# Three edits in a grouped-query attention and ResMLP kernel: twelve products moved from GpSimd to VectorE, two weight blocks sent through DRAM, one transpose placed a step later

## The chip, the cores and the metric

The kernel runs on one core of one Trainium2 chip. The metric is the device time of one execution in microseconds (us); the median of several executions is compared. The core's engines are TensorE (PE in the profile, with its weight loads as PEld), VectorE (DVE), ScalarE (ACT), GpSimd (POOL) and SyncE (SP). SP and POOL issue nearly all DMAs, each in its own order.

## The reference

Eight batches of 384 tokens. Attention has 16 query heads on 4 key and value heads of 64 elements; its output, 1024 wide, goes through a ResMLP block whose hidden layer is 4096 wide. The types in and out are float32.

```python
scores = scale * q @ k.T              # each query head on its group's key head
x = softmax(scores) @ v               # heads side by side: (8, 384, 1024)
a1 = alpha1 * x + beta1
tok = einsum('ts,bsd->btd', w_tok, a1)
u = x + lam * tok
a2 = alpha2 * u + beta2
ch = maximum(a2 @ w_ch1, 0) @ w_ch2   # (1024 x 4096), then (4096 x 1024)
out = u + lam * ch
```

## The kernel before, in words

**Pairs and products.** The batches are taken two at a time, in four pairs (`pair(i)`, L772). The two batches of a pair are the two block rows of a 2x2 block product, and each channel product is made of seven half-size products `o` = 1 to 7 instead of eight. The operands are sums and differences of blocks. `opb(k)` (L91) holds the left operands (turned activations and their sums, made by `sums_a`, L446, and at L850). `sum_w1(g, o)` (L506) makes the W1 operands on VectorE out of a left block `g` and a right block `g + 16`. The sums of W2 blocks are made once, in pair 0 (`sum_w2`, L496), written to DRAM as `w2s` (`keep_w2`, L493) and fetched by the later pairs (`fetch`, L525).

**Streams of weights.** A W1 block is 256 columns of W1, 512 KB as bf16. `load_w1` (L181) takes a free slot of the ring `w1` (six slots) and issues a DMA on POOL that casts float32 to bf16 on its way. `order1` (L439) is 0, 16, 1, 17, 2, 18 and so on: left and right blocks in turn. `queue` (L572 to L581) lists every load in order; `pump` (L534) issues the head of it each time `free` (L530) returns a slot. So a load is issued when the reader of an older block is through, in the queue's order alone.

**What runs in pair 0.** The attention of batches 0 and 1 comes first, then pair 0's first product (`first_product`, L641; matmuls at L681), then its second product (`second_product`, L728; matmuls at L752). The second product has 21 turns `(o, ms)`, a turn being 16 matmuls of 512 columns that end in one 128 x 512 accumulator, given out in four steps of four: 84 steps. While it runs, the attention of batches 2 and 3 is placed between its steps by hand: `plan` (L1069) says which calls follow which step of which product, `side(b)` (L214) gives the tables of one batch (L410 to L416), and batch 3's table is moved by 38 steps (L1122). Per pair of heads `p` these calls are `scores3` (scores at L260, exponentials on ACT at L269), `av` (matmuls at L295; on VectorE the reciprocal at L300, the division at L303 and the product with alpha1 and lam at L309), `tok_flip` (token mixing at L324 and L328; u at L331, a2 at L334; a store of u at L227) and, for batch 3, `turn` (L394: three transposes on TensorE at L398, copied by ACT at L400). Scores, `av`, `tok` and `turn` share three PSUM banks in rotation (`three`, L192), so each call waits until the reader of the bank three calls earlier is through.

**The order on the engines** is the program's order on each engine; nothing is reordered. A waiting instruction holds all behind it on its engine or queue.

**The lam products.** When a turn of the second product gives a finished 128 x 512 float32 block, `later` gets an entry; `flush` (L793) takes entries at later steps (L760 in the second product of pair 0, L845 in the next first product). An entry is `scaled` (L788): a `tensor_tensor` that multiplies the block in place with `lam_t` (L790) and a `store` (L441) that adds it to `out` by a DMA on POOL (L442). The multiply is on GpSimd in pair 0 (`lead`), twelve times, and on VectorE in the other pairs.

**After pair 0's second product** come pair 1's first product (matmuls at L831) and the rest in the same way. Group `g` of a first product needs W1 blocks `g` and `g + 16`. `home(c)` (L468) is a part of `arena` that holds block `c` of one quarter of W2 ("11") in pair 0's second product; its last readers are the turns of `o` = 7, which end with step 71, and the stretch is written again by pair 1's hidden units of group 6.

Of the kernel before, what the change touches and what calls it, by code (L numbers as in the profile page):

```python
# [13 lines left out]
def kernel(  # L14
# [21 lines left out]
    nc = tc.nc  # L36
# [82 lines left out]
    w2s = [tc.dram_tile([P, NDT * CW * P], bf, name=f"w2s{i}") for i in range(SLOTS)]  # L119
    PLACE2 = {o: i for i, o in enumerate((1, 2, 6, 5, 3, 7, 4))}  # L120
# [58 lines left out]
    w1_slots, w1_free = {}, list(range(RING))  # L179

    def load_w1(c):  # L181
        w1_slots[c] = w1_free.pop(0)
        nc.gpsimd.dma_start(out=w1[:, w1_slots[c]], in_=w1src[:, :, c * CW * P:(c + 1) * CW * P])  # L183
# [30 lines left out]
    def side(b):  # L214
# [197 lines left out]
        for p in range(NP):  # L412
            put((4, 10, 14, 18, 24, 29, 33, 35)[p], av, p)
            put((8, 15, 17, 22, 27, 32, 36, 38 if b % 2 else 39)[p], tok_flip, p)
            if by_pe(p):
                put(((13, 20, 22, 28, 34, 37, 40, 42) if b == 3 else (0, 0, 0, 0, 0, 36, 39, 41))[p], turn, p)  # L416
# [89 lines left out]
    def sum_w1(g, o):  # L506
        a, c = w1[:, w1_slots[g]], w1[:, w1_slots[g + NCH // 2]]
        H1, H2 = slice(0, NDT // 2), slice(NDT // 2, NDT)
        if o == 7:
            tt(out=c[:, H1], in0=c[:, H2], in1=c[:, H1], op=SUB)  # L510
            tb[g, 7], tb[g, 1], tb[g, 2], tb[g, 3] = c[:, H1], a[:, H1], a[:, H2], c[:, H2]
            return
        tb[g, o] = t = piece().rearrange("p (a c) -> p a c", a=NDT // 2)
        x, y = {5: (c[:, H1], a[:, H1]), 6: (c[:, H2], tb.get((g, 5))), 4: (a[:, H2], tb.get((g, 6)))}[o]
        tt(out=t, in0=x, in1=y, op=SUB)
# [61 lines left out]
    queue += [(load_w1, c) for c in order1[:4]]  # L577
    for i in range(1, NB):
        heads = [(load_w1, c) for c in order1[:4]] if i + 1 < NB else []
        queue += [(load_w1, c) for c in order1[4:]] + [(fetch, i, n) for n in range(SLOTS - 2)] + heads[:2]  # L580
# [191 lines left out]
    def pair(i):  # L772
# [15 lines left out]
        def scaled(o, b, ms, dw, t):  # L788
            if o != 2 or not last:
                (nc.gpsimd if lead else nc.vector).tensor_tensor(out=t, in0=t, in1=lam_t[:, dw * 512:(dw + 1) * 512], op=MUL)  # L790
            store(b, ms, dw, t)
# [26 lines left out]
        for g in range(NH // 2):  # L818
            X, Y, snap = {}, {}, {}
            for k, (o, e) in enumerate(SEQ1):  # L820
# [26 lines left out]
                if (o, e) in ((2, 1), (3, 1)):  # L847
                    free(w1_slots.pop(g if o == 2 else g + NCH // 2))
# [98 lines left out]
    with tc.manual_schedule(engines=order):  # L947
# [150 lines left out]
        for c in range(4):  # L1098
# [10 lines left out]
            put(0, 1, (61, 64, 68, 71)[c], last_w2, c)  # L1109
        for u, o in ((77, 5), (79, 7), (81, 6)):  # L1110
# [103 lines left out]
```

## Time and profile before

| | |
|---|---|
| median of three runs | 733.9 us (733.42 to 741.46) |
| the profiled execution, its own time | 731.92 us |
| its span (first to last instruction) | 729.9 us |
| TensorE busy, instructions | 717.4 us (98%), 5716 matmuls |
| VectorE busy | 543.9 us (75%) |
| ScalarE busy | 373.8 us (51%) |
| GpSimd busy | 199.2 us (27%) |
| DMA traffic of the core | 153.26 MB, mean 210 GB/s |
| pair 0's second product | 128.1 to 234.4 us |
| pair 1's first product | from 234.4 us |

Times in the views are microseconds from the span's start. In a line of the timeline the columns are the start, the duration of the group, the engine, the source line, the operation, `out<-in` by the program's names, the operand forms and the count; brackets give how long the engine was idle before it, and what ended that. "Busy" for TensorE counts pipelined matmuls whose ends overlap. A DMA's "landing" is the time from its issue to its completion.

### The profile page before, as it was taken

How to read it: one execution, taken by the hardware profiler on the slowest of the kernel's cores; microseconds unless marked ns; L12 is line 12 of the kernel's file. 1: busy time of each engine (PE TensorE's matmuls, PEld its weight loads, DVE VectorE, ACT ScalarE, POOL GpSimd, SP SyncE). 2: the span in 40 equal slices, each digit the busy share in tenths (PEclk: the TensorE clock that was granted, in tenths of full speed). 3: DMA queues.
4: the chain of work that ended last, by engine and by line, in shares of the span. 5: the costliest groups of instructions: out<-in, count | busy, mean ns of one | idle time of the engine just before them, and what ended most of it. 6: DMA issues, size and time to landing. Idle time of an engine off the chain costs nothing.

```text
span 729.9 us, 14511 instructions
## 1 busy us (share of the span) xinstructions
PE 717.4 (98%) x5716; PEld 408.7 (56%) x5716; DVE 543.9 (75%) x1009; ACT 373.8 (51%) x566; POOL 199.2 (27%) x242
## 2 busy tenths in 40 slices
PE   8899999999999999999999999999999999999998
PEld 4665555555555666555555566655555566654444
DVE  7888876577888988649678888748868988763354
ACT  7877666544563666643433466663333366650000
POOL 8844233221046551201022344200002222000011
PEclk9999999999999999999999999999999999999999
DMA  9999999999999999969989999998989999937965
GB/s 164 180 239 231 190 195 227 226 242 235 366 312 232 179 182 196 234 221 207 272 193 220 160 162 194 212 227 201 270 233 183 210 126 146 165 123 264 302 174 104
DMA packets 197616, 153.26 MB, mean 210 GB/s; under 512 B 90540, under 2 KB 175892, under 8 KB 197292
## 3 DMA queue, kind: packets, MB, share of 16 engines
q0 software_dynamic: 109872, 64.47, 65.4%
q1 hardware_dynamic: 86988, 87.42, 42.8%
q8 instruction: 44, 0.72, 0.4%
q10 hardware_dynamic: 688, 0.46, 0.2%
q14 instruction: 24, 0.20, 0.1%
HBM read 155.23 MB, written 39.85 MB: 267 GB/s over the span
## 4 chain that ended last, share of the span: by engine, by line
PE 90%; DVE 4%; POOL 2%; DMA 1%; issue 1%; ACT 1%; DVEq 0%; ACTq 0%; POOLq 0%
PE C L897 30%; PE X L831 17%; PE C L752 10%; PE Y L831 9%; PE Z L831 4%; PE sc L260 4%; PE X L681 4%; PE sc L295 3%; PE sc L324 3%; PE Y L681 3%; DMA ops<-obuf 1%; DVE pad L565 1%; PE Z L681 1%; PE tok L324 1%; POOL obuf L334 0%
## 5 line engine op out<-in xcount | busy, mean ns | idle before, releaser
L897 PE MATMUL C<-w,arena 128*128 128x512 bf16 (+2 forms) x744 | 168.3, 372 | 0.0
L269 ACT ACTIVATE es<-sc 128x1024 bf16<-128x1024 f32 x108 | 104.1, 1024 | 116.0 <-PE sc L260 107.6
L897 PEld LDWEIGHTS <-arena 128*128 128x128 bf16 x1040 | 94.8, 98 | 100.5 <-issue 5.1
L442 POOL DMA_DIRECT2D out_dram<-hT x45 | 40.0, 888 | 294.7 <-DVE hT L790 135.9
L836 ACT ACTIVATE hT<-X,bias 128x384 f32<-128x384 f32 x144 | 83.6, 582 | 60.0 <-PE X L831 55.2
L831 PEld LDWEIGHTS <-w 128*128 128x128 bf16 x768 | 75.1, 98 | 50.0
L831 PEld LDWEIGHTS <-pad 128*128 128x128 bf16 x576 | 56.4, 98 | 37.2
L183 POOL DMA_DIRECT2D w<-in_moe_w_ch_dram x48 | 45.4, 1002 | 105.6 <-PE X L831 36.5
L831 PE MATMUL X<-ops,w 128*128 128x384 bf16 x384 | 70.3, 326 | 0.0
L831 PE MATMUL X<-ops,pad 128*128 128x384 bf16 x384 | 70.3, 326 | 0.0
L897 PE MATMUL C<-pad,arena 128*128 128x512 bf16 (+2 forms) x296 | 70.2, 373 | 0.0
L324 PEld LDWEIGHTS <-wtokT 128*128 128x128 bf16 x576 | 39.0, 98 | 16.4 <-issue 3.4
L752 PEld LDWEIGHTS <-arena 128*128 128x128 bf16 x336 | 29.8, 98 | 30.0 <-issue 2.5
L331 DVE TENSOR_TENSOR xr<-sc,xr 128x384 f32<-128x384 f32 x48 | 26.5, 553 | 25.6 <-PE sc L324 14.3
L752 PE MATMUL C<-w,arena 128*128 128x512 bf16 x168 | 41.2, 379 | 0.0
L838 DVE TENSOR_TENSOR arena<-Y,hT 128x384 bf16<-128x384 f32 x48 | 26.5, 556 | 17.7 <-ACT hT L836 16.0
L295 PEld LDWEIGHTS <-es 128*128 128x128 bf16 x864 | 32.8, 97 | 11.3
L831 PE MATMUL Y<-ops,w 128*128 128x384 bf16 x192 | 39.1, 326 | 0.0
L831 PE MATMUL Z<-ops,w 128*128 128x384 bf16 x192 | 39.0, 326 | 0.0
L269 ACT ACTIVATE hT<-sc 128x1024 bf16<-128x1024 f32 x36 | 35.8, 1031 | 4.3 <-PE sc L260 4.0
L260 PE MATMUL sc<-qT,kT 64*128 64x384 bf16 (+2 forms) x504 | 37.2, 271 | 0.5 <-ACT hT L269 0.2
L842 ACT ACTIVATE arena<-X,bias 128x384 bf16<-128x384 f32 x48 | 27.9, 582 | 17.7 <-PE X L831 16.1
(190 smaller groups left out, 1175.1 us busy)
## 6 DMA issues: line engine op xcount, KB each, us to landing
w<-w2s SPq DMA_DIRECT2D x67, 512.0 KB, 5.1
w<-in_moe_w_ch_dram POOLq DMA_DIRECT2D x65, 512.0 KB, 9.8
pad<-w2s SPq DMA_DIRECT2D x25, 512.0 KB, 6.9
out_dram<-hT POOLq DMA_DIRECT2D x45, 256.0 KB, 7.1
out_dram<-xr SPq DMA_DIRECT2D x48, 192.0 KB, 5.3
q_raw<-in_q_dram POOLq DMA_DIRECT2D x28, 192.0 KB, 9.5
w2s<-w SPq DMA_DIRECT2D x10, 512.0 KB, 7.6
arena<-in_moe_w_ch_dram POOLq DMA_DIRECT2D x8, 512.0 KB, 15.9
```

Of the source, the lines that this page charges most:

```text
L183: nc.gpsimd.dma_start(out=w1[:, w1_slots[c]], in_=w1src[:, :, c * CW * P:(c + 1) * CW * P])
L260: nc.tensor.matmul(out=sc[:, hh, k % 4:k % 4 + n], lhsT=kT_[r, 2 * p // G, BLK[hh][sk], :], rhs=qT_[r, p, st:st + n, :], start=True, stop= ...
L269: nc.scalar.activation(out=e, in_=sc, func=EXP, scale=scale_qk)
L295: nc.tensor.matmul(out=av[:, hh, sq, :], lhsT=ess[k // 4][:, m % 2, k % 4, :], rhs=vb[:, sk, hk, :], start=(sk == 0), stop=(sk == NST - 1))
L324: nc.tensor.matmul(out=ps[:, tt, :], lhsT=wtokT[:, st, tt * P:(tt + 1) * P], rhs=a1s[p][:, st, :], start=(st == 0), stop=(st == NST - 1 an ...
L442: nc.gpsimd.dma_start(out=by_tok(out[b])[:, ms, dw * 512:(dw + 1) * 512], in_=o, accum_op=ADD)
L681: nc.tensor.matmul(out=ps[:, :n], lhsT=tb[G, o][:, dt, e * P:(e + 1) * P], rhs=opb(FIRST1[o], n)[:, dt], start=(o in (1, 2, 7) and dt == 0 ...
L752: nc.tensor.matmul(out=x, lhsT=lead_hid[:, t, FIRST2[o], ms * P:(ms + 1) * P], rhs=rhs[:, t % 4 * 512:(t % 4 + 1) * 512], start=(o in (1, ...
L831: nc.tensor.matmul(out=ps, lhsT=tb[g, o][:, dt, e * P:(e + 1) * P], rhs=opb(LEFT1[o])[:, dt], start=(o in (1, 2, 7) and dt == 0), stop=(dt ...
L836: nc.scalar.activation(out=snap[o, e], in_=ps, func=IDENT, bias=hi if o == 5 else lo)
L842: nc.scalar.activation(out=hid[:, t, 4], in_=ps, func=RELU, bias=hi)
L897: nc.tensor.matmul(out=x, lhsT=hid[:, t, LEFT2[o], ms * P:(ms + 1) * P], rhs=rhs[:, t % 4 * 512 + c0:t % 4 * 512 + c1], start=((not last o ...
```

## The change

Three edits:

- `scaled` multiplies on VectorE in every pair, so pair 0's twelve products leave GpSimd. They keep their place in the program's order, now in VectorE's stream.
- The W1 blocks at places 3 and 4 of `order1` (block 17, right, of group 1, and block 2, left, of group 2) of pair 1 do not go through the ring. `cast_w1` casts each from DRAM to a DRAM tile `w1s` on POOL after steps 15 and 17 of pair 0's second product; `back_w1` fetches it on SP, after steps 76 and 77, into `home(0)` and `home(1)`. The queue's ring loads for pair 1 are then places 0, 1, 2, 5, 6 and so on. `w1_at` says where a block lies, and `free_w1` frees a slot only for blocks that have one.
- For batch 3, `turn` of `p` = 2 comes after table step 23 instead of 22, where it stood just ahead of `tok` of `p` = 3.

On GpSimd's stream this gives, in the second product: store, cast, store, cast, three W2 loads, store, three W1 loads, six stores, three W1 loads. On VectorE's stream six lam products stand near the second product's end: one on either side of a `sum_w2`, one behind each of the last two `av` groups, one behind `tok` of `p` = 6 and one behind the first three operations of `sums_a`. On SP's stream the first fetch stands behind the last but one store of u, the second behind the last.

```diff
+    w1s = [tc.dram_tile([P, NDT * CW * P], bf, name=f"w1s{i}") for i in range(2)]
...
-    w1_slots, w1_free = {}, list(range(RING))
+    w1_slots, w1_at, w1_free = {}, {}, list(range(RING))
 
     def load_w1(c):
         w1_slots[c] = w1_free.pop(0)
-        nc.gpsimd.dma_start(out=w1[:, w1_slots[c]], in_=w1src[:, :, c * CW * P:(c + 1) * CW * P])
+        w1_at[c] = w1[:, w1_slots[c]]
+        nc.gpsimd.dma_start(out=w1_at[c], in_=w1src[:, :, c * CW * P:(c + 1) * CW * P])
+
+    def cast_w1(i, c):
+        nc.gpsimd.dma_start(out=w1s[i].rearrange("p (a c) -> p a c", a=NDT), in_=w1src[:, :, c * CW * P:(c + 1) * CW * P])
+
+    def back_w1(i, c, at):
+        w1_at[c] = at.rearrange("p (a c) -> p a c", a=NDT)
+        nc.sync.dma_start(out=at, in_=w1s[i])
+
+    def free_w1(c):
+        if c in w1_slots:
+            free(w1_slots.pop(c))
...
-                put(((13, 20, 22, 28, 34, 37, 40, 42) if b == 3 else (0, 0, 0, 0, 0, 36, 39, 41))[p], turn, p)
+                put(((13, 20, 23, 28, 34, 37, 40, 42) if b == 3 else (0, 0, 0, 0, 0, 36, 39, 41))[p], turn, p)
...
-        a, c = w1[:, w1_slots[g]], w1[:, w1_slots[g + NCH // 2]]
+        a, c = w1_at[g], w1_at[g + NCH // 2]
...
-    queue += [(load_w1, c) for c in order1[:4]]
+    queue += [(load_w1, c) for c in order1[:3]]
...
-        queue += [(load_w1, c) for c in order1[4:]] + [(fetch, i, n) for n in range(SLOTS - 2)] + heads[:2]
+        queue += [(load_w1, c) for c in order1[4 if i > 1 else 5:]] + [(fetch, i, n) for n in range(SLOTS - 2)] + heads[:2]
...
-                (nc.gpsimd if lead else nc.vector).tensor_tensor(out=t, in0=t, in1=lam_t[:, dw * 512:(dw + 1) * 512], op=MUL)
+                nc.vector.tensor_tensor(out=t, in0=t, in1=lam_t[:, dw * 512:(dw + 1) * 512], op=MUL)
...
-                    free(w1_slots.pop(g if o == 2 else g + NCH // 2))
+                    free_w1(g if o == 2 else g + NCH // 2)
...
+        for i, u in enumerate((15, 17)):
+            put(0, 1, u, cast_w1, i, order1[3 + i])
+            put(0, 1, 76 + i, back_w1, i, order1[3 + i], home(i))
```

## The prediction, made before the changed kernel ran

> **What bounds the kernel now.** I read the page first, then the busy time by stretches, then TensorE's timeline where a stretch is not full, then VectorE's and GpSimd's beside it, and last the lam products and DMA landings one by one.
>
> ```profile
> PE 717.4 (98%) x5716; PEld 408.7 (56%) x5716; DVE 543.9 (75%) x1009; ACT 373.8 (51%) x566; POOL 199.2 (27%) x242
> PEclk9999999999999999999999999999999999999999
> ```
>
> TensorE is busy 717.4 of 729.9 us at the full granted clock. Only its idle time can be won.
>
> ```profile
> 180.00:204.00 24.00, 24.00 (x229) 13.19 (x228) 19.52 (x30) 13.14 (x20) 0.91 (x1) 1.00 1.02 368
> 204.00:234.40 30.40, 28.62 (x268) 16.25 (x267) 27.72 (x43) 15.56 (x24) 16.08 (x16) 1.00 1.16 270
> 234.40:300.00 65.60, 65.60 (x405) 39.51 (x404) 55.79 (x99) 43.50 (x72) 29.07 (x35) 1.00 1.36 192
> ```
>
> The first number behind a stretch is its length, the second TensorE's busy time, the fourth VectorE's, the sixth GpSimd's. TensorE is full before 204 and from 234.4; between them, the end of pair 0's second product, it lacks 30.40 - 28.62 = 1.78 us, while VectorE works 27.72 of 30.40 us. That is the most this change can win there. TensorE's timeline names the three gaps:
>
> ```profile
> 203.97 0.33 PE L398 MATMUL sc<-ident,obuf 128*128 128x128 bf16 x3
> 204.89 0.33 PE L324 MATMUL sc<-a,wtokT 128*128 128x128 bf16 x3 [0.59 <-ACT es L269]
> ...
> 221.20 0.33 PE L398 MATMUL sc<-ident,obuf 128*128 128x128 bf16 x3 [0.24 <-ACT es L269]
> ...
> 222.78 1.03 PE L752 MATMUL C<-w,arena 128*128 128x512 bf16 x4
> 224.76 0.34 PE L324 MATMUL sc<-a,wtokT 128*128 128x128 bf16 x3 [0.95 <-DVE a L309]
> ```
>
> 0.59 us: `tok` waits for a PSUM bank that an exponential still reads. 0.24 us: the same for a `turn`. 0.95 us: `tok` waits for VectorE's L309. VectorE, then GpSimd, before the last one:
>
> ```profile
> 220.26 0.69 DVE L767 TENSOR_TENSOR hT<-C,hT 128x512 f32<-128x512 f32 x1 [0.39 <-ACT hT L764]
> 220.87 2.02 DVE L499 TENSOR_TENSOR w<-w,pad 128x2048 bf16<-128x2048 bf16 x1
> 222.81 0.18 DVE L300 RECIPROCAL rinv<-sc 128x6 f32<-128x6 f32 x1
> ...
> 223.62 1.08 DVE L309 TENSOR_TENSOR a<-xr,vecs 128x384 bf16<-128x384 f32 x1
> ...
> 238.07 0.69 DVE L515 TENSOR_TENSOR pad<-w 128x1024 bf16<-128x1024 bf16 x1 [2.92 <-DMA w<-in_moe_w_ch_dram]
> 238.68 0.95 DVE L850 TENSOR_TENSOR ops<-ops 128x1536 bf16<-128x1536 bf16 x1
> ```
>
> ```profile
> 220.24 1.55 POOL L790 TENSOR_TENSOR hT<-hT,vecs 128x512 f32<-128x512 f32 x1
> 222.09 0.88 POOL L442 DMA_DIRECT2D out_dram<-hT  x1 [0.30 <-POOL hT L790]
> 222.71 1.57 POOL L790 TENSOR_TENSOR hT<-hT,vecs 128x512 f32<-128x512 f32 x1
> ```
>
> L499 takes 1.22 us elsewhere (217.00: 1.21) and 2.02 here, L309 0.56 elsewhere and 1.08 here; a GpSimd lam product runs beside both. The same operation on either engine:
>
> ```profile
> L790 DVE TENSOR_TENSOR hT<-hT,vecs x30: 679/684/693, 328.6 to 716.4; 128x512 f32<-128x512 f32 x30
> L790 POOL TENSOR_TENSOR hT<-hT,vecs x12: 1263/1559/2112, 142.8 to 263.6; 128x512 f32<-128x512 f32 x12
> ```
>
> **The lam products.** Twelve leave GpSimd (median 1.559 us) and cost VectorE 0.684 each; back to back 0.61 (L767 of the same size starts at 220.26, the next at 220.87). Between 212 and 228 six come: 6 x 0.61 = 3.7 us added. The stretched rows there go: L334 at 212.75 (1.77 for 0.56), L309 at 216.14 (0.93), L499 at 220.87, L309 at 223.62 and 225.44 (1.74): 1.21 + 0.37 + 0.80 + 0.52 + 1.18 = 4.1 us. So VectorE's load is even; what counts is where the time lies. I follow it from 216.14: L309 without its stretch ends at 216.7, lam to 217.3, L499 to 218.5, lam to 219.1, L331 and L334 to 220.2, inside the 0.39 us of idle before L767, which starts at 220.26 as now. L499 then ends near 222.0, L300 and L303 follow, L309 ends at 223.3. TensorE can want it at 224.76 - 0.95 = 223.81. That gap closes: 0.95 us. The next L309, with one lam product ahead, ends at 225.3; its `tok` comes at 227.33 - 0.95 = 226.4. If TensorE is 0.59 us early by then (below), all these times move together, since each wait in the chain is for TensorE.
>
> Three early lam products (after 142.79, 147.67, 164.28) can hold VectorE back for ACT's copy L764. The first two copies are done (142.7, 147.6) before VectorE is there; the third ends at 164.2, so the next L300 slips from 165.15 to 165.8, its L309 to 167.1, and `tok` is at 168.43: nothing. The three in pair 1 (246 to 264) lie where TensorE is full and replace stretches (L863 1.43 for 0.56 at 246.57 and at 254.69): nothing either; without that cover they would cost 3 x 0.61 = 1.8 us. A store now waits on VectorE instead of GpSimd; the last of the six then goes near 232, so the three W1 loads behind it leave POOL near 233, for blocks wanted after 242: nothing.
>
> **The transpose a step later.** `tok` takes the bank that `turn` took without waiting at 203.97; `turn` comes after `tok` and four matmuls, 203.97 + 0.67 + 0.86 = 205.5, and its bank was free at 204.89. The 0.59 us go. On ACT the copy into the accumulator (L744) now stands ahead of `turn`'s copy, 0.4 us earlier; `turn`'s bank is wanted again only at the scores of 209.65. A loss here is bounded by the 0.59 itself.
>
> **The sum.** 0.59 + 0.95 = 1.54 us. The 0.24 stays, since the turn, copy and exponential ahead of it shift together. The profiled execution gives 731.92 - 1.54 = 730.4. It lies 1.98 under the median of 733.9, so on the median's footing 732.4.
>
> **The two W1 blocks.** TensorE full from 234.4 leaves nothing to win after it, but a block that is late can take back the 1.54. `sum_w1(1, 5)` needs block 17; now it lands at 238.04 and holds VectorE 2.92 us; then L850 makes the operand for `o` = 3, which TensorE reads at 240.23, 0.6 us later. Shifted, that is 238.69, so the block must land by 238.69 - 0.61 - 0.95 = 237.1. The fetch stands on SP behind the store of `p` = 6, whose L331 on VectorE ends near 226.5 by the chain above (two lam products ahead of it), 225.9 with the 0.59, plus 0.57 for the store's issue: 226.5. Bounds for its landing: 5.1 us, the median of SP's `w<-w2s`, same size; 10.0 us, SP's `w2s<-w` issued at 222.92. So 231.6 to 236.5: in time, with 0.6 to spare at the late end. I take 7 us, between `w<-w2s` in this product (7.4 at 162.20) and into `pad` (6.7 at 189.73): 233.5, while VectorE gets there near 234.4, its end of the L515 before, shifted by 0.59. By the Trainium skill (DMA: Bandwidth & Descriptors, Anatomy of one DMA) a DMA takes about 2.0 us plus its bytes at 436 GB/s; as an estimate from that page 512 KB would take 3.2 us and this wait could never bind. The rows here are two to three times that, so the rows decide. Block 2, fetched behind the last store, is wanted a whole group (9 us) later: nothing.
>
> The casts cost POOL 0.8 us of issue each (L479), in an idle stretch: POOL waits 7.5 us for TensorE before 158.47; without that idle time they would delay the loads by 1.6 us. They cost DMA time. Nearest rows: L479 lands in 10.2 to 18.7 us, median 12.4. Cast two goes out near 152.3 and lands at 162.5 to 171; the W2 loads issued at 158.47, 159.87 and 160.73 queue behind it. The last lands at 173.51 now, TensorE reads it at 176.91: 3.4 us spare. At 12.4 us the cast is off the engines about when the first load's data (landing 164.26) needs them, so I take zero. Bounds: zero, and both casts whole ahead of the loads, about 4 us each by the spacing of those landings (169.46 to 173.51).
>
> **Rivals.**
> 1. *The fetch comes too late.* For: the 10.0 us row, and SP's order behind VectorE. Against: SP's landings of 5.1 to 7.4. If block 17 lands as late as now (238.04), L850 ends 0.9 us after TensorE wants it: -1.54 + 0.9, 733.3. At 13.7 us, the longest landing of a W1 load (L183): 240.2, wait 3.1, 735.5.
> 2. *Slower: the casts hold up W2.* Place: the read at 176.91. It decides once the last W2 load slips more than 3.4 + 1.54 = 4.9 us. With both casts whole ahead, 8.1 us late: wait 4.7, 733.9 - 1.54 + 4.7 = 737.1. For: DMA share 1.04 already between 145 and 160. Against: POOL issues no load in those 7.5 us. By the skill (same page, Queues, rings and completion order) each DMA engine takes turns between queues packet by packet, so SP's traffic would stretch the casts; no run here shows these casts yet.
> 3. *One of the two gaps stays.* The reordered bank wait comes back one call later, or VectorE reaches L309 late for a reason that I don't see: -0.95 or -0.59, 733.0 to 733.3. Against: the margins of 0.6 and 0.5 us above.
>
> **How the numbers follow.** Forecast 0.58; rival 1 0.17; rival 2 0.10; rival 3 0.15. The time is 732.4. Low end: all 1.78 us won on the profiled execution's own footing, 730.1. High end: rival 1's late end, 735.5; that leaves out rival 2 and little else. A measurement here tells about 2% (14.7 us) from no change; no case comes near it, so faster 0.01, same 0.96, slower 0.03 for a stall that repeats where I priced one.
>
> **What would show it.** Right: no gap on TensorE before L324 near 204 and 223; L499 and L309 back at 1.22 and 0.56 throughout 212 to 226; pair 1's first product starting near 232.9; block 17's fetch landing before 234.4 and L515 no longer waiting for a DMA. Wrong: a wait of TensorE for L850's `ops` or for a W2 load near 176, or a `tok` still waiting for L309.

## The result, and the profile after

The changed kernel takes 740.35 us (median of 21 runs, 737.35 to 749.26); the kernel before takes 733.42 us beside it (21 runs, 731.02 to 742.48). The ratio is 1.0094, with a 95% interval of 1.007 to 1.0118: some 6.9 us slower, where 1.5 us faster was forecast. The profiled execution took 738.47 us with a span of 736.7 us, 6.8 us more than before.

First, where in the run the time went. The start of each stage is its first matmul in TensorE's timeline; the differences are worked out.

| stage | before | after | difference |
|---|---|---|---|
| up to pair 0's second product | 128.1 us | 127.8 us | -0.3 us |
| pair 0's second product | 106.3 us | 110.8 us | +4.5 us |
| pair 1's first product | 72.8 us | 75.3 us | +2.5 us |
| everything behind it | 422.7 us | 422.8 us | +0.1 us |

The loss lies in the two stages that the edits touch. Busy time of the whole kernel, from the page, shows nothing of it: TensorE is still at 98%, GpSimd is 17.9 us less busy and VectorE no busier than before.

```profile
PE 719.5 (98%) x5716; PEld 409.2 (56%) x5716; DVE 542.0 (74%) x1021; ACT 374.0 (51%) x566; POOL 181.3 (25%) x230
PEclk9999999999999999999999999999999999999999
```

Busy time by stretches, with the columns as before (the second number is TensorE's, the fourth VectorE's):

```profile
160.00:180.00 20.00, 18.76 (x192) 10.71 (x192) 13.95 (x24) 12.07 (x16) 2.01 (x3) 1.00 1.20 214
180.00:204.00 24.00, 24.00 (x226) 13.26 (x226) 19.88 (x31) 11.80 (x18) 0.04 (x1) 1.00 0.98 325
204.00:238.60 34.60, 30.26 (x279) 16.82 (x276) 27.20 (x47) 17.01 (x26) 8.46 (x10) 1.00 1.16 303
238.60:300.00 61.40, 59.22 (x364) 35.48 (x363) 49.78 (x95) 39.39 (x65) 21.22 (x27) 1.00 1.39 188
```

TensorE lacks 1.24 us between 160 and 180, 4.34 between 204 and the second product's end, and 2.18 in pair 1. The first and the last were full before. Its timeline names what it waited for:

```profile
176.86 0.39 PE L273 MATMUL sc<-qT,kT 64*128 64x256 bf16 x4 [0.58 <-DVE xr L316]
177.92 0.39 PE L273 MATMUL sc<-qT,kT 64*128 64x128 bf16 x4 [0.66 <-DVE xr L344]
...
208.61 0.59 PE L765 MATMUL C<-arena 128*128 128x512 bf16 x2 [1.44 <-DVE arena L512]
...
211.93 0.59 PE L765 MATMUL C<-arena 128*128 128x512 bf16 x2 [1.75 <-DVE arena L512]
...
226.54 0.33 PE L411 MATMUL sc<-ident,obuf 128*128 128x128 bf16 x3 [0.24 <-ACT es L282]
...
242.08 0.81 PE L844 MATMUL X<-ops,pad 128*128 128x384 bf16 x4 [0.72 <-ACT hT L849]
...
245.00 0.81 PE L844 MATMUL X<-ops,pad 128*128 128x384 bf16 x4 [1.46 <-ACT hT L849]
```

(L273, L316, L344, L512 and L765 of the changed kernel are L260, L303, L331, L499 and L752 before; L411 is L398, L844 and L849 are L831 and L836.) The two gaps of the forecast are gone: no wait ahead of `tok` (now L337) is left. The 0.24 us stay. The others are new (two more, of 0.20 and 0.71 us at 213 and 215 us, are left out here), and each names VectorE or ScalarE. That is where a first reading stops; VectorE's and ScalarE's own timelines show what these two waited for:

```profile
176.25 0.56 DVE L316 TENSOR_TENSOR xr<-sc,rinv 128x384 f32<-128x384 f32 x1 [3.31 <-DMA out_dram<-xr]
...
207.33 1.23 DVE L512 TENSOR_TENSOR arena<-pad,arena 128x2048 bf16<-128x2048 bf16 x1 [3.49 <-DMA w2s<-arena]
210.65 1.23 DVE L512 TENSOR_TENSOR arena<-pad,arena 128x2048 bf16<-128x2048 bf16 x1 [2.10 <-DMA w2s<-arena]
...
235.98 0.68 DVE L803 TENSOR_TENSOR hT<-hT,vecs 128x512 f32<-128x512 f32 x1
...
241.16 0.69 DVE L528 TENSOR_TENSOR pad<-arena,w 128x1024 bf16<-128x1024 bf16 x1 [0.83 <-DMA arena<-w1s]
```

```profile
244.37 1.05 ACT L849 ACTIVATE hT<-X,bias 128x384 f32<-128x384 f32 x2 [2.33 <-DMA out_dram<-hT]
```

All three are waits for a store to be through before its source is written again: a store of u (3.31 us), stores of the W2 sums (6.1 us over four waits), a store of an output block (2.33 us). Two of these stores are SP's, one is POOL's. So the question is why SP's and POOL's stores are late. SP's timeline, after and before:

```profile
153.35 3.57 SPq L350 DMA_TRANSPOSE ops<-obuf  x1
...
158.14 3.94 SPq L350 DMA_TRANSPOSE ops<-obuf  x1
...
162.85 5.10 SPq L350 DMA_TRANSPOSE ops<-obuf  x1
...
183.21 0.55 SPq L240 DMA_DIRECT2D out_dram<-xr  x1
...
185.20 0.54 SPq L507 DMA_DIRECT2D w2s<-w  x1
```

```profile
152.76 2.13 SPq L337 DMA_TRANSPOSE ops<-obuf  x1
...
156.11 1.23 SPq L337 DMA_TRANSPOSE ops<-obuf  x1
...
158.11 1.24 SPq L337 DMA_TRANSPOSE ops<-obuf  x1
...
176.26 0.97 SPq L227 DMA_DIRECT2D out_dram<-xr  x1
...
178.67 0.53 SPq L494 DMA_DIRECT2D w2s<-w  x1
```

Batch 2's attention turns its result by DMA transposes on SP (L350, before L337: `a2_transpose`; batch 3 does it on TensorE by `turn`). Each held SP 1.23 to 2.13 us here before and 3.57 to 5.10 us after. Over the 14 transposes of this stretch the sum is 25.8 us before and 37.6 after: the 8 of `obuf` go from 13.0 to 23.1, the 6 of q and k from 12.9 to 14.5. The lines behind them go out 6.95 us (183.21 against 176.26) and 6.53 us later. The casts are what runs beside them: they were issued at 144.94 and 150.93 and landed 13.1 and 14.1 us later, near 158.0 and 165.1.

```profile
L188 POOL DMA_DIRECT2D w1s<-in_moe_w_ch_dram x2: 1207/1232/1257, 144.9 to 150.9; - x2
DMA to landing us min/median/max: 13.1/13.6/14.1
```

The other store is POOL's. Its last one waits for the last lam product:

```profile
236.96 0.84 POOL L455 DMA_DIRECT2D out_dram<-hT  x1 [2.95 <-DVE hT L803]
```

It goes out 1.6 us before pair 1 starts at 238.6; before it went out at 227.05, 7.35 us ahead of pair 1. It lands at 244.28, and ScalarE's L849, which writes the same part of `hT`, starts at 244.37. In the kernel before, the store and ScalarE's write of that part (L836) stand so:

```profile
227.05 0.87 POOL L442 DMA_DIRECT2D out_dram<-hT  x1 [0.30 <-POOL hT L790]
```

```profile
237.23 1.18 ACT L836 ACTIVATE hT<-X,bias 128x384 f32<-128x384 f32 x2 [0.72 <-PE X L831]
```

That store landed at 234.60, so the write at 237.23 did not wait for it.

That gives two theories, for two parts of the loss. A: the casts make SP's DMA transposes hold SP longer; SP's stores come late, and VectorE waits to write their sources (loss in the second product). B: six lam products placed behind attention work on VectorE make the last output store late; ScalarE waits to write its source (loss in pair 1). Rivals: C, the fetches, not the casts, cost it (the prediction's first rival); D, the casts delay POOL's W2 loads (its second); E, the turned transpose placed later costs it.

### The profile page after: what moved, and what is told of

The parts are those of the page before. It is cut to its first block, busy times and chain, and to the rows that moved or that the text cites. A ratio compares the mean times of both kernels' runs of the same rounds, so it can differ in the third digit from the quotient of the medians.

```text
span 736.7 us, 14500 instructions
## 1 busy us (share of the span) xinstructions
PE 719.5 (98%) x5716; PEld 409.2 (56%) x5716; DVE 542.0 (74%) x1021; ACT 374.0 (51%) x566; POOL 181.3 (25%) x230
## 4 chain that ended last, share of the span: by engine, by line
PE 82%; DMA 6%; DVE 5%; POOL 3%; issue 2%; ACT 1%; SPq 1%; DVEq 0%; ACTq 0%; POOLq 0%
PE C L910 30%; PE X L844 17%; PE Y L844 8%; PE C L765 5%; PE Z L844 4%; PE sc L273 4%; PE X L694 4%; PE Y L694 3%; PE sc L308 3%; PE sc L337 3%; DMA w2s<-arena 2%; DMA out_dram<-xr 2%; DMA ops<-obuf 1%; DMA out_dram<-hT 1%; DVE pad L578 1%
## 5 line engine op out<-in xcount | busy, mean ns | idle before, releaser
L849 ACT ACTIVATE hT<-X,bias 128x384 f32<-128x384 f32 x144 | 83.6, 581 | 62.4 <-PE X L844 55.4
L844 PEld LDWEIGHTS <-w 128*128 128x128 bf16 x736 | 72.0, 98 | 47.9
L844 PEld LDWEIGHTS <-pad 128*128 128x128 bf16 x576 | 56.3, 98 | 39.8 <-issue 2.6
L844 PE MATMUL X<-ops,pad 128*128 128x384 bf16 x384 | 70.4, 326 | 2.2 <-ACT hT L849 2.2
L844 PE MATMUL X<-ops,w 128*128 128x384 bf16 x368 | 67.3, 326 | 0.0
L765 PEld LDWEIGHTS <-arena 128*128 128x128 bf16 x336 | 29.8, 97 | 33.6 <-issue 6.4
L337 PEld LDWEIGHTS <-wtokT 128*128 128x128 bf16 x576 | 39.1, 98 | 15.0 <-issue 3.3
L344 DVE TENSOR_TENSOR xr<-sc,xr 128x384 f32<-128x384 f32 x48 | 26.5, 553 | 22.4 <-PE sc L337 14.4
L765 PE MATMUL C<-w,arena 128*128 128x512 bf16 x168 | 41.2, 379 | 0.0
L273 PE MATMUL sc<-qT,kT 64*128 64x384 bf16 (+2 forms) x504 | 37.9, 272 | 2.4 <-DVE xr L316 1.3
L282 ACT ACTIVATE hT<-sc 128x1024 bf16<-128x1024 f32 x36 | 35.7, 1032 | 4.0 <-PE sc L273 3.9
L844 PE MATMUL Y<-ops,w 128*128 128x384 bf16 x184 | 37.4, 326 | 0.0
L844 PE MATMUL Z<-ops,w 128*128 128x384 bf16 x184 | 37.4, 326 | 0.0
```

The costliest lines, as they stand in the source:

```text
L273: nc.tensor.matmul(out=sc[:, hh, k % 4:k % 4 + n], lhsT=kT_[r, 2 * p // G, BLK[hh][sk], :], rhs=qT_[r, p, st:st + n, :], start=True, stop= ...
L282: nc.scalar.activation(out=e, in_=sc, func=EXP, scale=scale_qk)
L337: nc.tensor.matmul(out=ps[:, tt, :], lhsT=wtokT[:, st, tt * P:(tt + 1) * P], rhs=a1s[p][:, st, :], start=(st == 0), stop=(st == NST - 1 an ...
L765: nc.tensor.matmul(out=x, lhsT=lead_hid[:, t, FIRST2[o], ms * P:(ms + 1) * P], rhs=rhs[:, t % 4 * 512:(t % 4 + 1) * 512], start=(o in (1, ...
L844: nc.tensor.matmul(out=ps, lhsT=tb[g, o][:, dt, e * P:(e + 1) * P], rhs=opb(LEFT1[o])[:, dt], start=(o in (1, 2, 7) and dt == 0), stop=(dt ...
L849: nc.scalar.activation(out=snap[o, e], in_=ps, func=IDENT, bias=hi if o == 5 else lo)
```

## The experiments

Ratios are to the kernel before on the same chip, with 95% intervals. "Second" and "first" are the lengths of pair 0's second and pair 1's first product in the profiled execution, taken as in the table above (before 106.3 and 72.8 us, after 110.8 and 75.3).

| run | ratio (95%) | second | first |
|---|---|---|---|
| the W1 edit alone | 1.0125 (1.0083 to 1.0166) | 113.6 | 72.8 |
| the lam edit alone | 1.0074 (1.0043 to 1.0105) | 105.1 | 77.2 |
| the turn edit alone | 1.0017 (0.9986 to 1.0048) | 113.0 | 72.8 |
| lam and turn | 1.0039 (1.0013 to 1.0064) | 104.6 | 77.0 |
| lam and turn, products handed out earlier | 1.0014 (0.9994 to 1.0034) | 105.1 | 74.3 |
| the whole change, products earlier | 1.0119 (1.0086 to 1.0152) | 111.9 | 73.0 |
| before, plus casts nobody reads | 1.012 (1.0096 to 1.0144) | 113.6 | 73.7 |
| the whole change, casts 29 steps later | 1.007 (1.0049 to 1.0092) | 109.1 | 74.8 |
| casts nobody reads, near 200 us | 1.0099 (1.0073 to 1.0125) | 107.7 | 79.1 |
| batch 2 turned on TensorE | 1.0019 (0.9994 to 1.0044) | 108.7 | 72.8 |
| the same, plus casts nobody reads | 1.0032 (1.0001 to 1.0062) | 109.0 | 72.8 |
| lam early, turn, blocks loaded straight | 1.0006 (0.9978 to 1.0033) | 105.1 | 75.1 |
| the whole change, batch 2 on TensorE | 1.0023 (0.9989 to 1.0057) | 106.2 | 74.5 |
| the same, products earlier | 0.9995 (0.9969 to 1.002) | 106.6 | 72.8 |

Five of these profiled executions have a stretch inside one of the two stages in which the granted TensorE clock is 0.50: 3.41 us from 179.8 in the W1 edit alone, from 214.1 in the turn edit alone, from 188.3 in the whole change with products earlier and from 242.8 with the casts near 200 us; 6.83 us from 180.7 in the kernel before plus casts nobody reads. Each begins within 1.1 us of the end of a wait of TensorE. At half the clock at most half of such a stretch is lost: by this estimate up to 1.7 or 3.4 us of these five lengths are not waits. In the other rows, in the kernel before and in the changed kernel the clock is 1.00 in both stages. What starts such a stretch is not shown.

### The edits one at a time

The W1 edit alone: the changed kernel with the lam and turn edits taken back.

```diff
-                nc.vector.tensor_tensor(out=t, in0=t, in1=lam_t[:, dw * 512:(dw + 1) * 512], op=MUL)
+                (nc.gpsimd if lead else nc.vector).tensor_tensor(out=t, in0=t, in1=lam_t[:, dw * 512:(dw + 1) * 512], op=MUL)
...
-                put(((13, 20, 23, 28, 34, 37, 40, 42) if b == 3 else (0, 0, 0, 0, 0, 36, 39, 41))[p], turn, p)
+                put(((13, 20, 22, 28, 34, 37, 40, 42) if b == 3 else (0, 0, 0, 0, 0, 36, 39, 41))[p], turn, p)
```

> The casts and the fetches of the two W1 blocks alone; lam products on GpSimd and the transpose as before. Theory A (the casts load the DMA engines, SyncE's queue falls about 7 us behind in its transposes, VectorE waits for SyncE's stores, TensorE for VectorE: 5.3 us of idle time in the changed kernel between 176 and 216): slower than before by 4 to 7 us, with VectorE waiting for out_dram<-xr near 173 and for w2s<-arena near 207. Theory B (the lam products overload VectorE, which works 27.7 of 30.4 us there): within 1 us of before.

Measured: 741.78 us beside 732.9, ratio 1.0125: 8.9 us slower, more than the 4 to 7 expected. The whole loss is in the second product (+7.3 us, in which the 3.41 us at half the clock lie and the two gaps of the forecast stay open), and pair 1's first product is as before. VectorE waits 4.5 us for a store of u and 3.8 us for stores of W2 sums. The W1 edit alone costs no less than the whole change.

The lam edit alone: the kernel before, with

```diff
-                (nc.gpsimd if lead else nc.vector).tensor_tensor(out=t, in0=t, in1=lam_t[:, dw * 512:(dw + 1) * 512], op=MUL)
+                nc.vector.tensor_tensor(out=t, in0=t, in1=lam_t[:, dw * 512:(dw + 1) * 512], op=MUL)
```

> The twelve lam products on VectorE alone. Theory A: no wait for SyncE's stores; the 0.95 us gap near 224 closes; but the last store of the six goes 10 us later, and ScalarE's write to hT in pair 1 waits for its landing, up to 2.2 us of TensorE's time as in the changed kernel: -1 to +1.5 us against before. Theory B: slower than before by 4 us or more, with TensorE waiting for VectorE between 176 and 216.

Measured: 738.03 us, ratio 1.0074: 5.1 us slower, where -1 to +1.5 were expected. In the profiled execution the second product gains 1.2 us, and the next stage loses 4.4; 3.5 us more lie outside these two stages and are not explained. The waits of the next stage:

```profile
DVE pad L515 <- DMA w<-in_moe_w_ch_dram: 6.0, 1, 6.0
PE X L831 <- DVE ops L850: 3.4, 1, 3.4
ACT hT L836 <- DMA out_dram<-hT: 0.8, 1, 0.8
```

The columns are the sum, the number and the longest. Without the W1 edit the late stores cost through another wait: block 17's ring load goes out on POOL right behind them, at 234.26 (the last store at 233.70), and lands 8.83 us later; before, it went out 5.05 us behind the last store and landed in 5.95. VectorE waits 6.0 us for it. So moving the lam products costs more in pair 1 than the gaps that it closes, with or without the W1 edit; only the wait that ends last differs.

The turn edit alone:

```diff
-                put(((13, 20, 22, 28, 34, 37, 40, 42) if b == 3 else (0, 0, 0, 0, 0, 36, 39, 41))[p], turn, p)
+                put(((13, 20, 23, 28, 34, 37, 40, 42) if b == 3 else (0, 0, 0, 0, 0, 36, 39, 41))[p], turn, p)
```

> The transpose of p = 2 one step later, alone. Both theories: the 0.59 us gap near 204 closes and nothing else moves: -0.6 us, within 0.5.

Measured: 733.99 us, ratio 1.0017 with 1 inside the interval; the expected -0.6 us is inside it too, so the run can't tell a gain of that size from none. E falls as the cause of the 6.9 us. The run's profiled execution took 740.24 us, 6.3 us above its median, and can't be used for the median's stages: in it SP's 14 transposes took 35.7 us (one of them 6.69) and VectorE waited 7.7 us for stores of W2 sums, with no cast from DRAM to DRAM in the kernel. So the same stall can arise in a single execution without these casts.

### The lam products, and where they are handed out

Both edits without the W1 edit: the two diffs above, on the kernel before.

> The change without the two W1 blocks: lam products on VectorE and the transpose a step later. Theory A: -1.54 us from the two gaps, up to +2.2 us from the late store: -1.5 to +0.7 us against before. Theory B: slower than before by 4 us or more.

Measured: 736.0 us, ratio 1.0039: 3.1 us slower, where +0.7 was expected at the most. Both forecast gaps are closed (the second product takes 104.6 us, 1.7 less), and the stage behind loses 4.2 us to the same wait for block 17.

```profile
DVE pad L515 <- DMA w<-in_moe_w_ch_dram: 5.3, 1, 5.3
PE X L831 <- DVE ops L850: 2.3, 1, 2.3
```

Then the same with the entries of `later` handed out from turn 15 on instead of 17:

```diff
-                    if t % 8 == 3 and later and (later[0][1] == 1 or k > 16 and later[0][1] != 4):
+                    if t % 8 == 3 and later and (later[0][1] == 1 or k > 14 and later[0][1] != 4):
```

> Lam products on VectorE and the transpose a step later, no casts, and the six lam products taken two turns earlier (from turn 15 instead of 17), so that their stores go before the last W1 loads are due. Theory A (what costs without the casts is the late last store, with the W1 load of block 17 behind it on GpSimd's queue): the wait of 2 to 3 us for L850's operand goes, and the two gaps stay closed: -1 to -2 us against before. Rival (VectorE is too full between 204 and 213 for products there): as without the shift, 1 to 4 us slower than before, with TensorE waiting for VectorE between 204 and 225.

Measured: 734.33 us beside 733.07, ratio 1.0014, the interval reaching from 0.9994; 1 to 2 us faster than before was expected. Handing the products out earlier gives back much of the loss: the first product takes 74.3 us instead of 77.0. VectorE still waits 4.9 us for block 17, of which TensorE sees 1.3. B is borne out in direction: what matters is when the last product, and so the last store, goes.

The whole change with this earlier hand-out:

```diff
-                    if t % 8 == 3 and later and (later[0][1] == 1 or k > 16 and later[0][1] != 4):
+                    if t % 8 == 3 and later and (later[0][1] == 1 or k > 14 and later[0][1] != 4):
```

> The whole change with the six lam products taken two turns earlier. Theory A: TensorE's 2.2 us near 243 (ScalarE's wait for the last store) go, the waits from the casts stay: 4 to 6 us slower than before. Rival (the late store is an effect of VectorE's delay by the casts, not of the products' place): as the changed kernel, about 7 us slower.

Measured: 742.32 us, ratio 1.0119. The wait in pair 1 is gone (first product 73.0 instead of 75.3 us), as B says; the casts' part is all there (second product 111.9). The time is nevertheless no better than the whole change's 1.0094, where it should have been some 2 us better. The two ratios' intervals overlap. The second product's +5.6 us against +4.5 hold the 3.41 us at half the clock, which the changed kernel's execution does not have; so these lengths do not show a larger part of the casts. Why the median is not better stays open.

### The casts, with nobody reading them

The kernel before with the two casts issued after the same steps, into DRAM tiles that nothing reads; all W1 blocks still come through the ring.

```diff
+    w1s = [tc.dram_tile([P, NDT * CW * P], bf, name=f"w1s{i}") for i in range(2)]
...
+    def cast_w1(i, c):
+        nc.gpsimd.dma_start(out=w1s[i].rearrange("p (a c) -> p a c", a=NDT), in_=w1src[:, :, c * CW * P:(c + 1) * CW * P])
...
+        for i, u in enumerate((15, 17)):
+            put(0, 1, u, cast_w1, i, order1[3 + i])
```

> The kernel before plus the two casts after steps 15 and 17, whose result nobody reads: no fetch, all W1 blocks through the ring, lam products on GpSimd, transpose as before. Theory A (the casts' DMA traffic holds up SyncE's queue): slower than before by 4 to 9 us, as with the blocks in use, with VectorE waiting for out_dram<-xr near 173 and for w2s<-arena near 205. Rival (the fetches or the block's new place cost the time): within 1 us of before.

Measured: 742.47 us, ratio 1.012, the same as the W1 edit alone. C falls: without any fetch the whole loss is there. SP's transposes are stretched in the same way, 37.3 us for the 14.

```profile
L341 SPq DMA_TRANSPOSE ops<-obuf x8: 1242/2338/5284, 142.3 to 189.5; - x8
```

```profile
DVE xr L307 <- DMA out_dram<-xr: 5.8, 1, 5.8
PE sc L264 <- DVE xr L307: 3.1, 1, 3.1
DVE arena L503 <- DMA w2s<-arena: 1.9, 1, 1.9
```

D falls as well: no wait for a W2 load is among them. In the changed kernel the three loads landed at 169.26, 172.72 and 176.34, and TensorE reads the last of them from 178.24.

Then I moved the casts of the whole change in time:

```diff
-        for i, u in enumerate((15, 17)):
+        for i, u in enumerate((44, 46)):
```

> The changed kernel with the casts after steps 44 and 46 (near 187 us) instead of 15 and 17, when SyncE issues no transposes and GpSimd waits for nothing. Theory A (what costs is that SyncE's transposes take longer beside the casts): TensorE's waits near 176 and 208 to 215 go, the 2.2 us near 243 for the last store stay: within 2 us of before. Rival (the casts' share of the DMA engines costs wherever they are, and SyncE's writes of w2s fill the engines between 180 and 200): slower than before by 4 us or more, the waits of VectorE for w2s<-arena stay.

Measured: 737.89 us, ratio 1.007: 4.8 us slower, where less than 2 was expected. The premise failed: nothing that POOL does there waits for step 44, so the casts went out near 166 us, 37.7 us into the second product, still beside transposes of SP. Here it is those of q and k that are stretched: the last three took 5.51, 3.21 and 3.74 us (4.51, 1.29 and 1.24 before), while the 8 of `obuf` took 12.6 us (13.0 before). SP ran 5 us late. The waits at 176 us are gone, those of L512 remain (1.50 and 1.62 us of TensorE). It tells that the harm moves with the casts to the transposes beside them, and no more than that.

To get them clear of the transposes, I put the unread casts behind the first W1 load, near 200 us (the diff is against the run with unread casts):

```diff
-        for i, u in enumerate((15, 17)):
+        for i, u in enumerate((50, 54)):
```

> The kernel before plus the two unused casts behind GpSimd's first W1 load, so that they are issued near 199 us, after SyncE's last transpose of the stretch. Theory A: SyncE has no lag at its first store of a W2 sum, the W2 side is as before; the W1 loads behind the casts land up to 8 us later, which can cost up to 3 us near 230 to 240. Rival (casts slow every DMA): SyncE's stores of W2 sums near 200 to 205 are late by 4 us or more, with VectorE waiting for w2s<-arena, 4 us or more slower than before.

Measured: 740.39 us, ratio 1.0099: 7.1 us slower, where up to 3 were expected. SP's part is nearly gone, as A says: its 14 transposes take 27.3 us (25.8 before), SP runs 1.6 us late instead of 6.8, and VectorE's wait for stores of W2 sums is 2.4 us (1.1 before). But the cost moved to POOL's own DMAs:

```profile
DMA to landing us min/median/max: 20.0/23.1/26.2
```

```profile
DVE pad L519 <- DMA w<-in_moe_w_ch_dram: 9.7, 2, 8.8
...
ACT hT L840 <- DMA out_dram<-hT: 6.1, 3, 4.6
...
PE X L835 <- ACT hT L840: 4.4, 2, 3.9
```

The first line is the casts' landing. All that POOL issues behind them lands in the order of issue: a W1 load at 211.79, the casts at 220.48 and 227.42, the next W1 loads at 231.56 and 235.03. By these spacings a cast from DRAM to DRAM takes 6.9 to 8.7 us of the queue, and a load of the same block into SBUF 3.5 to 4.1. Stores then land 15 to 21 us after their issue.

### Batch 2's transposes taken off SP

This is the experiment for A itself: leave the casts where they are, and take away what they stretch. Batch 2 turns its result on TensorE, as batch 3 does, with batch 3's table; SP then has 6 transposes left in the stretch instead of 14.

```diff
-            return b in (0, 3) or b % 2 and p >= NP - (4 if first else 3)
+            return b in (0, 2, 3) or b % 2 and p >= NP - (4 if first else 3)
...
-                put(((13, 20, 22, 28, 34, 37, 40, 42) if b == 3 else (0, 0, 0, 0, 0, 36, 39, 41))[p], turn, p)
+                put(((13, 20, 22, 28, 34, 37, 40, 42) if b in (2, 3) else (0, 0, 0, 0, 0, 36, 39, 41))[p], turn, p)
```

First without casts, for the price of the 24 added transposes on TensorE:

> The partner of the run with casts: the kernel before with batch 2's eight transposes of a2 on TensorE, no casts. 24 more matmuls of 128 columns and eight more bank turns: 1 to 3 us slower than before by both theories.

Measured: 733.79 us beside 733.28, ratio 1.0019: 0.5 us slower by the medians, where 1 to 3 were expected. In the profiled execution the second product takes 108.7 us, 2.4 more, of which the gaps are 0.6 (2.36 us instead of 1.78): the added matmuls cost about 1.8 us.

With the unread casts added (the diff of the casts above):

> The kernel before plus the two unused casts, and batch 2's eight transposes of a2 taken from SyncE's DMA queue to TensorE (as batch 3's are): SyncE has 6 transposes instead of 14 between 138 and 185 us. Theory A (SyncE's DMA transposes take longer beside the casts, 37 us instead of 26 for fourteen, and all SyncE does later waits behind them): SyncE's first store of a W2 sum comes no more than 3 us later than in the same kernel without casts (7 us with the transposes on SyncE), VectorE's wait of 3 to 6 us for out_dram<-xr near 175 goes, and the kernel is at most 2 us slower than its partner without casts. Rival (the casts slow every DMA of that stretch by their share of the engines): 6 us or more of lag, the wait stays, 5 us or more slower than its partner.

Measured: 734.36 us, ratio 1.0032. The casts are the same: they land in 12.8 to 14.0 us (13.1 and 14.1 in the changed kernel). With all 14 transposes on SP they cost 742.47 - 733.07 = 9.4 us; with 6 left, 734.36 - 733.79 = 0.6 us. Not all of the 9.4 us need be waits: of the five executions the one with a mean granted clock of 1.00 took 738.93 us, 5.9 more, and the other four, at a mean of 0.995 to 0.998, 741.77 to 743.02. No wait of VectorE for a store of u is left. The six remaining transposes are still stretched, 16.8 us against 12.5, and SP falls 2.5 us behind instead of 6.8; VectorE's waits for SP's stores stay at 0.8 us. A holds.

### The blocks without a bounce

If the casts are the harm, the two blocks could be loaded straight into `home(0)` and `home(1)` on POOL once the turns of `o` = 7 are through, with the lam products handed out early:

```diff
+    def home_w1(c, at):
+        w1_at[c] = at.rearrange("p (a c) -> p a c", a=NDT)
+        nc.gpsimd.dma_start(out=w1_at[c], in_=w1src[:, :, c * CW * P:(c + 1) * CW * P])
...
+        for i in range(2):
+            put(0, 1, 72 + i, home_w1, order1[3 + i], home(i))
```

> Lam products on VectorE two turns earlier, the transpose a step later, and the two W1 blocks loaded straight into their places in arena by GpSimd's casting DMA after steps 72 and 73, when the last readers of these places are through: no bounce through DRAM, no added traffic, and block 17 asked for near 224 us instead of 232. Theory A (the two gaps close, what took the gain back without casts was the wait for block 17): TensorE's idle time of this stretch goes from 1.78 to 0.3 us: -1 to -1.6 us against before. Rival (VectorE too full before 225 or the last stores late again): 0 to 3 us slower than before.

Measured: 733.48 us beside 733.28, ratio 1.0006 (0.9978 to 1.0033): no gain, where 1 to 1.6 us were expected. The second product takes 105.1 us (1.2 less), and pair 1 loses 2.3 us.

```profile
DVE pad L524 <- DMA arena<-in_moe_w_ch_dram: 5.8, 1, 5.8
...
PE X L840 <- DVE ops L859: 1.5, 1, 1.5
```

Block 17 is still too late. Its load goes out at 224.05, but POOL's DMAs land in their order, and four stores and a load ahead of it are not through: it lands at 238.93, 6.4 us after pair 1 starts (3.6 before).

### Both losses taken away

The whole change, with batch 2 on TensorE:

```diff
-            return b in (0, 3) or b % 2 and p >= NP - (4 if first else 3)
+            return b in (0, 2, 3) or b % 2 and p >= NP - (4 if first else 3)
...
-                put(((13, 20, 23, 28, 34, 37, 40, 42) if b == 3 else (0, 0, 0, 0, 0, 36, 39, 41))[p], turn, p)
+                put(((13, 20, 23, 28, 34, 37, 40, 42) if b in (2, 3) else (0, 0, 0, 0, 0, 36, 39, 41))[p], turn, p)
```

> The whole change, with batch 2's eight transposes of a2 on TensorE instead of SyncE. Theory A (the change's loss is two sums: the casts beside SyncE's transposes, and the late last store): the casts' part goes, so TensorE's waits near 176 and 208 to 215 (5.3 us) are under 1 us, the late store's 1 to 2.2 us near 243 stay, the transposes cost their own 1.4 us: 0 to 3 us slower than before instead of 7. Rival (with the lam products on VectorE the casts cost the same without SyncE's transposes, since VectorE has no slack): 5 us or more slower.

Measured: 734.0 us beside 732.85, ratio 1.0023: 1.2 us slower instead of 6.9. The waits at 176 and from 208 to 215 us are gone; B's is left and is all there is besides the 0.24 us:

```profile
ACT hT L849 <- DMA out_dram<-hT: 2.9, 2, 2.4
PE X L844 <- ACT hT L849: 1.5, 1, 1.5
```

And with the products handed out from turn 15 as well (`k > 14`, the diff shown above):

> As the run before, with the six lam products two turns earlier as well, so that neither loss is left. Theory A: TensorE's idle time from 120 to 260 us under 2.5 us, within 1.5 us of before, and no slower than the run before. Rival (early lam products cost as much on VectorE as the late store): 2 to 4 us slower than before, with TensorE waiting for VectorE near 215 to 225.

Measured: 732.03 us beside 732.85, ratio 0.9995 (0.9969 to 1.002). It is faster than the change and can't be told from the kernel before. Between 204 and 246 us two gaps are left on TensorE:

```profile
213.02 0.39 PE L273 MATMUL sc<-qT,kT 64*128 64x128 bf16 x4 [0.23 <-DVE xr L316]
...
224.14 0.33 PE L411 MATMUL sc<-ident,obuf 128*128 128x128 bf16 x3 [0.24 <-ACT es L282]
```

Against the kernel with batch 2 on TensorE alone, its second product takes 106.6 us instead of 108.7 and the first is the same: a gain of 2.1 us in the profiled executions (its TensorE gaps fall from 2.36 to 0.54 us). That is about the gain that the change was forecast to have, 1.5 us, once both losses are away; by the medians it is not shown, since the two ratios' intervals overlap. The 24 transposes on TensorE take about as much again, so the best version only equals the kernel before.

## Why the prediction was wrong

**Right: the two gaps and their working.** Both gaps ahead of `tok` closed, and the 0.24 us stayed. On VectorE a lam product took 0.685 us as priced (L803), L512 went back to 1.22 to 1.23 us throughout and L322 (before L309) to a mean of 0.558 us; VectorE's busy time stayed even (543.9 to 542.0 us). With the losses away the gain was there: the second product was 1.7 us shorter with lam and turn alone. The turn edit by itself cost nothing that can be measured.

**Nearly right: the fetch.** Block 17's fetch went out on SP at 232.35, 6.3 us before pair 1 starts; forecast were 6.4 (226.5 against 232.9). VectorE had it at 241.16, so it landed within 8.8 us (7 taken, bounds 5.1 and 10.0). VectorE waited 0.83 us for it, so the sign "L515 no longer waiting for a DMA" failed by that much; TensorE did not wait for it. The rows of the kernel before were the better guide: the estimate of 3.2 us that stood beside them was far too low. Rival 1's wait does occur, but as a wait for a ring load, in the three kernels that move the lam products without the W1 edit.

**Wrong, the larger step: "I take zero" for the casts.** The prediction priced them against POOL's W2 loads alone, and rival 2 put the harm at the read of 176.91, with SP's traffic only as something that would stretch the casts. For those loads zero was about right: the last landed 2.8 us later (176.34 against 173.51), and nothing waited for it. But the casts also stretch SP's traffic. The step that failed is the search for who is beside the casts. 144 to 165 us is where SP issues batch 2's DMA transposes; the 14 transposes of the stretch took 12 us more of SP's time (batch 2's 8 alone 10), SP fell 6.8 us behind, and VectorE waited for the sources of SP's stores. The largest loss alone was 9.4 us (the casts on the kernel before) and fell to 0.6 us without those transposes. SP's timeline of the kernel before, which the prediction does not show, could have warned of it: it has single transposes of 4.51 us (165.46) and 2.73 us (170.72) among those of 1.23, so their time was plainly not fixed. By the Trainium skill (DMA: Bandwidth & Descriptors, Queues, rings and completion order) each DMA engine takes turns between the queues that have work, packet by packet. From this it follows as much that the casts slow SP's traffic as the other way round; the prediction drew only the second conclusion. The trace agrees on the direction (37.6 us against 25.8); that this is how the casts make a transpose hold SP longer is not shown.

**Wrong, the size of a cast.** The upper bound for a cast's hold on POOL's queue was "about 4 us each by the spacing of those landings". The rows for it were loads into SBUF. Where casts stood in a row with such loads, a cast from DRAM to DRAM took 6.9 to 8.7 us, about twice its neighbours.

**Wrong, the smaller step: "the last of the six then goes near 232 … nothing".** The place was about right: the last product came 2.6 us before pair 1's start, where 0.9 was forecast. The price was not. The step looked at the W1 loads behind the store and not at the store's source. That part of `hT` is written again by ScalarE in pair 1's first product (now L849, before L836), 2.85 us after pair 1 starts. Before, that was at 237.23, and the last store had landed at 234.60: 2.6 us to spare. The store now goes out 5.7 us later against pair 1's start (1.6 us before it instead of 7.35), so some 3 us were to be waited for. ScalarE's write came 2.9 us later against pair 1's start than before; the profile counts only 2.33 of it as the wait for this store, because the store ahead, landed at 241.08, had already held ScalarE's write before. TensorE lost 2.2 us, 0.72 of it behind that earlier write. The spare time stood in the trace of before. In the kernels without the W1 edit the W1 loads behind the stores are late instead (5.3 and 6.0 us waited), so "nothing" was wrong for them as well.

**The chances.** The case that came, casts that do harm, had 0.10, at 737.1 us in another place; the lam products' late store had no case. The range, cut at rival 1, left both out.

**Open.** Why the casts make a transpose hold SP longer; why the whole change with early products is not faster than the change; what starts the same stall in a single execution without casts; and what sets the clock to 0.50 in some executions. The two long transposes at 169.35 and 173.91 (4.51 and 4.23 us) start when the casts have landed, beside the W2 loads that were issued behind these; which of the two held them is not told apart.

## What to carry to other kernels

An added DMA is costed against all queues that are busy in its window, the transposes of another engine's queue above all, and by the time until its neighbours' stores are through, since that is when their sources may be written again. When an operation ahead of a store is moved, follow the store to its landing and then to the next writer of its source: only what goes beyond the spare time there (2.6 us here) is paid for. A change that closes gaps of 1.5 us gains nothing if it takes more than that beyond the spare time elsewhere.

## What the runs showed of the hardware

SP's DMA transposes have no fixed issue time: over the whole of the kernel before they took 1.18 to 5.51 us. Beside casts from DRAM to DRAM on POOL more of them were long: the 14 of one stretch took 25.8 us without and 37.6 us with the casts. A 512 KB block cast from float32 to bf16 took 6.9 to 8.7 us of POOL's queue from DRAM to DRAM and 3.5 to 4.1 us into SBUF in the same stretch; one load into SBUF took 6.5 us by the same spacing in the kernel that loads the blocks straight (225.12 to 231.57), so the ratio is no constant. In the stretches read here POOL's DMAs landed in the order of their issue, so a backlog shows in all behind it: a store of an output block landed in 5.0 to 11.6 us in pair 0's second product before, in 15 to 21 behind the two casts near 200 us, and in up to 18.7 behind two W1 loads in the kernel that loads the blocks straight. A VectorE product of 128 x 2048 bf16 that took 2.02 us beside a GpSimd product took 1.22 to 1.23 us everywhere in that stage once GpSimd had none. In five of the profiled executions the granted TensorE clock was 0.50 for 3.41 or 6.83 us inside the two stages, each time beginning within 1.1 us of the end of a wait of TensorE.
